# Block-recurrent attention with a gated MLP on one core: the next batch's M sets in pairs over four banks, the states' read next to the next scores

## The chip, the cores and the metric

The kernel runs on one core of a Trainium2 chip. The metric is the device time of one execution in microseconds; before the change it is 742.33 us (median of three runs, 742.26 to 742.41). The profiled execution has a span of 740.4 us, and the times inside it are counted from its start.

## The reference

Eight batches of eight heads; 512 tokens and 32 states of 64 numbers per head; everything in float32. Tokens read states, states read tokens, and both results go through an MLP whose activation is h * erf(softplus(h)):

```python
scores = scale * x @ state^T            # (512 x 32) per head
a      = softmax(scores)                # over the 32 states
xread  = a @ state                      # 512 rows of the batch
a2     = softmax(scale * state @ x^T)   # over the 512 tokens
sread  = a2 @ x                         # 32 more rows of the batch
h      = concat(xread, sread) @ w_in    # 512 -> 2048 (rows: heads side by side)
out    = (h * erf(softplus(h))) @ w_out # 2048 -> 512
```

## The kernel before

**M sets.** For the token rows xread is never formed. Since h = a (state w_in), the kernel forms the small matrices M = state w_in, once per batch, and then h = M^T a^T. One *M set* (`mixed`, L372, by way of `mixed_part`, L377) covers 512 columns of one batch's M: eight small matmuls (L385), each with 64 rows of a head pair's half (e = 0, 1) and 32 columns for one head pair i, so that eight of them fill the 128x128 array as tiles of 64x32. The results of e = 0 and e = 1 lie in two banks of the pool `ps_at`, and are copied out by ScalarE (L387) and VectorE (L388). A batch has four sets.

**Scores and read.** The scores of a batch (`scored`, L190, matmuls at L197) use the same 64x32 tiles; they need the transposed x, made by VectorE in `turn_x` (L330), and two `ps_at` banks, which ScalarE empties (L207). The states' read (`read_tokens`, L264) multiplies the turned token weights by x: 32 groups of matmuls 128 rows deep and 32 columns wide (L273) into one `ps_at` bank, which VectorE empties (L279). The weights for it come from an exponential on ScalarE (L246), and from VectorE's L248, L249 and L356, after which DMAs turn blocks.

**Hidden and output products.** The MLP runs in fast (seven-product) block schemes. `hidden7` (L437) forms a group of h from seven block products (L457, each four matmuls of 128 columns) in two banks p, q of the pool `ps_h`, then again in two more; ScalarE copies (L468, L473) and VectorE's additions (L465) empty them. Then come softplus (L464) and Erf (L507) on ScalarE and the multiplication by h on VectorE (L508). `project7` (L544) needs sums of these (S1 to S4, L559 to L562, VectorE) and adds up output blocks with matmuls of 256 columns (L563) in the four banks of `ps_o`; `store7` (L567) empties them with a copy on ScalarE (L574) and additions on VectorE (L573), and stores. `combine_m` (L397 to L400) and `combine_a` (L428 to L431) prepare sums of M and of the weights on VectorE; in batch 1 `combine_w` (L539) does so for w_out.

Accumulators: `ps_at` has two banks, `ps_h` two, `ps_o` four[...].

**The order.** From batch 1 on, each batch has four groups g. The matmuls of group g's `hidden7` and those of the previous group's `project7` are interleaved; `project7` is a generator that yields every second product of 256 columns, and `side` is a table from the number of such a step to small work put in at that point. With this table the next batch's attention is threaded in: `turn` is a generator over the stages of `attention` (scores; states' weights; token weights; normalisation and turning; read, with the load of the next x). Within this the tile scheduler may shift instructions a little; every engine then runs its own list in order. `behind` says that instructions are to be issued after the marked ones.

In the kernel before, group 0 of a batch has the batch's own read at step 2 and the next batch's scores at step 6, and groups 2 and 3 have one M set each at step 4 and at step 8.

Of the kernel before, what the change touches and what calls it, by code (L numbers as in the profile page):

```python
# [8 lines left out]
F32 = mybir.dt.float32  # L9
# [7 lines left out]
def kernel(  # L17
# [17 lines left out]
    nc = tc.nc  # L35
    B, H, S, D = x.shape
    Ns = state.shape[2]
    d_model, d_ff = moe_w_in.shape
    P = 128
    NI = H // 2  # L40
# [15 lines left out]
    mix = ctx.enter_context(tc.tile_pool(name="mix", bufs=4))  # L56
    act = ctx.enter_context(tc.tile_pool(name="act", bufs=2))
    outs = ctx.enter_context(tc.tile_pool(name="outs", bufs=2))
    ps_at = ctx.enter_context(tc.tile_pool(name="ps_at", bufs=2, space=PSUM))
    ps_h = ctx.enter_context(tc.tile_pool(name="ps_h", bufs=2, space=PSUM))  # L60
# [45 lines left out]
    st = const.tile([P, B, P], F32, name="st")  # L106
    x_t[0] = xin.tile([P, NC, H, D], F32, name="x")
    for c in range(NC):
        (nc.scalar, nc.sync)[c % 2].dma_start(
            out=x_t[0][:, c], in_=x[0, :, P * c:P * c + P].rearrange("h p d -> p h d"))  # L110
# [11 lines left out]
    w_in = const.tile([P, NF // 2, NK, 2 * P], F32, name="w_in")  # L122
# [29 lines left out]
    gw = GF * P  # L152
# [35 lines left out]
    marks = []  # L188
# [13 lines left out]
    def scores(b, xT):  # L202
        s2 = scored(b, xT)
        on_pe = marks.pop()
        sc = att.tile([P, 2, S], F32, name="sc")
        for e in range(2):
            last = nc.scalar.copy(sc[:, e], s2[e])  # L207
        marks[:] = last, on_pe
        return sc, last

    def states_weights(b, sc, both):

        aT[b] = keep.tile([P, 2, S], F32, name="aT")
        a = both[:, 0:2].rearrange("p e (k n) -> p e k n", n=Ns)
        m1 = small.tile([P, 2, NC * NI], F32, name="m1")
        for e in range(2):
            nc.vector.transpose(out=both[:, e], in_=sc[e])
        for e in range(2):
            nc.vector.reduce_max(out=m1[:, e], in_=a[:, e], axis=AX.X)
        for e in range(2):  # L220
            nc.vector.tensor_tensor(a[:, e], a[:, e], over(m1[:, e]), op=ALU.subtract)
            nc.scalar.activation(out=a[:, e], in_=a[:, e], func=ACTF.Exp, scale=scale)
        return a
# [11 lines left out]
    def largest(sc):  # L235
        m2 = small.tile([P, 2], F32, name="m2")
        for e in range(2):
            nc.vector.reduce_max(out=m2[:, e:e + 1], in_=sc[:, e], axis=AX.X)
        nc.vector.tensor_scalar(m2, m2, -scale, None, op0=ALU.mult)
        return m2  # L240
# [20 lines left out]

    sn_t = {}

    def read_tokens(b, a2T, z2):  # L264


        xt = x_t.pop(b)
        sr = ps_at.tile([P, 2, D], F32, name="at")
        for e in range(2):
            for c in range(NC):  # L270
                for i in reversed(range(NI)):
                    q = slice(Ns * i, Ns * i + Ns)
                    nc.tensor.matmul(out=sr[q, e, :], lhsT=a2T[:, e, c, q],  # L273
                                     rhs=xt[:, c, 2 * i + e, :],
                                     start=(c == 0), stop=(c == NC - 1))
        sn = sn_t[b] = const.tile([P, 2, D], F32, name="sn0") if b == 0 else \
            st[:, b - 1, :].rearrange("p (e d) -> p e d", e=2)
        for e in range(2):
            nc.vector.tensor_scalar(sn[:, e], sr[:, e], z2[:, e:e + 1], None, op0=ALU.mult)  # L279
# [48 lines left out]
    def turn_x(b):  # L328
        xT = att.tile([P, NI, S], F32, name="xT")
        last = nc.vector.transpose(out=xT.rearrange("p i t -> p (i t)"),  # L330
                                   in_=xq_t.pop(b).rearrange("p i m d -> p (i m d)"))
        if b + 1 < B:
            load_xq(b + 1)
        return xT, last

    def attention(b, xT=None):

        turned = []  # L340
        if xT is None:
            xT, *turned = turn_x(b)
        sc, _ = scores(b, xT)
        marks.extend(turned)
        yield
        both = att.tile([P, NI, S], F32, name="xT")
        a = states_weights(b, [sc[:, e] for e in range(2)], both)
        yield
        z2 = weigh_tokens(sc, largest(sc), both[:, 2:4])
        yield  # L350
        normalise(a)
        for e in range(2):
            nc.vector.transpose(out=aT[b][:, e], in_=both[:, e])
        yield

        nc.vector.transpose(out=both[:, 0:2], in_=both[:, 2:4])  # L356
        a2T = att.tile([P, 2, NC, P], F32, name="sc")
        blocks = both[:, 0:2].rearrange("p e (c m n) -> p m (e c) n", m=NI, n=Ns)
        rows = a2T.rearrange("p e c (i n) -> p i (e c) n", n=Ns)
        for m in range(NI):  # L360
            for i in range(NI):
                nc.sync.dma_start(out=rows[Ns * m:Ns * m + Ns, i],
                                  in_=blocks[Ns * i:Ns * i + Ns, m])
        yield
        read_tokens(b, a2T, z2)
        if b + 1 < B:
            load_x(b + 1)
        yield

    m_t = {}  # L370

    def mixed(b, g, *copies):  # L372

        m_t[b, g] = mix.tile([P, 2, gw], F32, name="m")
        mixed_part(b, g, 0, 1, *copies)

    def mixed_part(b, g, j, parts, copy0=nc.scalar.copy, copy1=nc.vector.tensor_copy):  # L377
        n = gw // parts
        mg = m_t[b, g][:, :, n * j:n * j + n]
        fs = slice(2 * g + j, 2 * g + j + 2 // parts)  # L380
        ps = [ps_at.tile([P, gw], F32, name="at")[:, 0:n] for _ in range(2)]
        for i in range(NI):
            for e in range(2):
                r, q = slice(D * e, D * e + D), slice(Ns * i, Ns * i + Ns)
                nc.tensor.matmul(out=ps[e][q, :], lhsT=st[r, b, q],  # L385
                                 rhs=w_in[r, fs, i, :], start=True, stop=True)
        copy0(mg[:, 0], ps[0])  # L387
        copy1(mg[:, 1], ps[1])  # L388
# [248 lines left out]
    def behind(marks, f, *args):  # L637
        with ExitStack() as order:
            for m in marks:
                order.enter_context(tc.issue_after(m.ins))  # L640
            return f(*args)
# [183 lines left out]
    xT, _ = turn_x(1)  # L825
# [6 lines left out]
    turn = attention(1, xT)  # L832
# [38 lines left out]
    at = [combine_a(1)]  # L871
# [12 lines left out]
    for b in range(1, B + 1):  # L884
        if b < B:
            groups = fast(b, 2, lambda h, b=b: put_x(b, h))
        else:
            groups = fast(b, 1, lambda h: put_s)
        for g, (first, second) in enumerate(groups):
            side = {}  # L890
            if b < B and g == 0:
                side[2] = lambda turn=turn: next(turn)
            if 1 < b < B and g == 0:
                side[3] = lambda: behind(marks, combine_m, b, 1 - begins(b))
            if b + 1 < B:

                late = b == 1
                if g == late:
                    turn = attention(b + 1)
                    side[6] = lambda: behind(marks, next, turn)  # L900
                if g == 1 + late:
                    side[1] = lambda: next(turn)
                    side[7] = lambda: behind(marks, lambda: [next(turn) for _ in range(3)])
                if g > 1:
                    o = g - 2 ^ begins(b + 1)
                    side[4] = lambda: mixed(b + 1, 2 * o)
                    side[8] = lambda: mixed(b + 1, 2 * o + 1)
                    if g == 3:
                        side[6] = lambda: behind(marks, combine_a, b + 1)
                        side[3] = lambda: behind(marks, combine_m, b + 1, begins(b + 1))  # L910
            elif b + 1 == B and g == 1:
                side[4] = lambda: [turn_read(range(k, min(k + 4, B))) for k in range(0, B, 4)]
            elif b + 1 == B and g > 1:

                if g == 2:
                    side[6] = lambda: combine_a(B)
                side[8] = lambda: combine_s(g - 2 ^ begins(B))
            steps = accompanied(pending(), side)
            copy = [nc.vector.tensor_copy] if (b, g) == (1, 1) else []
            gT_ = first(lambda: next(steps), *copy)  # L920
            if b == 1 and g == 0:
                combine_m(1, 1 - begins(1))
                behind(marks, combine_w, begins(1), 1, 2)
            if b == 1 and g == 1:
                behind(marks, combine_w, begins(1), 4, 3)
            done(steps)
            if b == 1 and g == 1:
                behind(marks, combine_w, 1 - begins(1), 1, 2, 4, 3)

            def pending(gT=gT_, second=second):  # L930
                return second(gT)
# [31 lines left out]
```

## Time and profile before

| what | value |
|---|---|
| time, median of 3 | 742.33 us |
| span of the profiled execution | 740.4 us |
| DMA, mean over the span | 63 GB/s |
| granted TensorE clock | 1.0 throughout |
| L385, M sets with 512 columns | 448 matmuls, 601 ns each, 31.5 us of busy time |
| L273, reads | 512 matmuls, 220 ns each, 8.8 us |
| L197, scores | 128 matmuls, 658 ns each, 10.6 us |

The counts are of instructions: a float32 product is two of them, so an M set has 16. In the rows of the groups the mean of one is its length from start to end; small matmuls on different tiles run side by side, which is why 448 of 601 ns make only 31.5 us. "PE" is TensorE's matmuls and "PEld" its weight loads, "DVE" VectorE, "ACT" ScalarE. In the chain of waits a piece is a line's stretch of work with its count, without time in which it only waited for its engine; a number in brackets behind a row of a timeline is the idle time ahead of it and what ended it.

### The profile page before, as it was taken

The page shows a single profiled execution, that of the slowest core. Times are in us where ns is not written, and L with a number is a line of the kernel's source. Part 1 is how long each engine was busy: PE and PEld are TensorE (multiplying, and loading weights), DVE is VectorE, ACT ScalarE, POOL GpSimd, SP SyncE. Part 2 cuts the span into 40 slices and gives each one's busy share as a digit, 9 for nine tenths or more (in the row PEclk, how much of TensorE's full clock was granted, in tenths as well). Part 3 has the DMA queues.
Part 4 walks back from the last instruction along what each step waited for, and adds up shares of the span by engine and source line. Part 5 has one row for each costly group of instructions (what it writes and reads, how often), then busy time and mean ns, then how long its engine had stood idle before and what let it go on. Part 6 is the DMA issues. An engine that isn't in the chain of part 4 may idle for free.

```text
span 740.4 us, 12067 instructions
## 1 busy us (share of the span) xinstructions
PE 727.6 (98%) x4986; PEld 583.9 (79%) x4986; DVE 523.5 (71%) x765; ACT 396.9 (54%) x498; POOL 0.7 (0%) x6
## 2 busy tenths in 40 slices
PE   7899999999999999999999999999999999999997
PEld 6434435878889888988889888988898889999996
DVE  3987888898688666966598568966596656575423
ACT  3898884656456445654365445654565434443340
POOL 0000000000000000000000000000000000000000
PEclk9999999999999999999999999999999999999999
DMA  7468752331160203310061105110201000000001
GB/s 231 170 205 250 209 101 58 86 58 26 33 130 19 53 1 76 69 29 29 15 128 21 38 1 111 35 35 22 59 29 29 30 1 29 1 29 1 27 4 28
DMA packets 139166, 46.40 MB, mean 63 GB/s; under 512 B 126696, under 2 KB 130536, under 8 KB 139112
## 3 DMA queue, kind: packets, MB, share of 16 engines
q1 hardware_dynamic: 136744, 44.78, 24.1%
q10 hardware_dynamic: 2368, 0.85, 0.5%
q8 instruction: 39, 0.64, 0.4%
q14 instruction: 15, 0.12, 0.1%
HBM read 33.03 MB, written 8.91 MB: 57 GB/s over the span
## 4 chain that ended last, share of the span: by engine, by line
PE 85%; DVE 2%; ACT 1%; issue 0%
PE o L563 49%; PE h L457 26%; PE at L385 4%; PE o L513 3%; PE h L673 1%; PE at L197 1%; PE at L273 1%; DVE s L508 1%; ACT s L507 0%; DVE hs L465 0%; ACT L507 0%; DVE raw L539 0%; DVE xT L356 0%; DVE ot L573 0%; PE at L285 0%
## 5 line engine op out<-in xcount | busy, mean ns | idle before, releaser
L464 ACT ACTIVATE s<-hs 128x512 f32<-128x512 f32 x120 | 75.4, 630 | 81.5 <-DVE hs L465 81.1
L563 PE MATMUL o<-w_out,s 128*128 128x256 f32 x480 | 118.2, 380 | 0.6 <-DVE s L508 0.4
L563 PE MATMUL o<-raw,hs 128*128 128x256 f32 x480 | 116.2, 384 | 0.0
L563 PE MATMUL o<-w_out,hs 128*128 128x256 f32 x480 | 114.8, 380 | 0.0
L563 PEld LDWEIGHTS o<-raw,hs 128*128 128x128 f32 x480 | 89.1, 190 | 32.0 <-issue 21.0
L563 PEld LDWEIGHTS o<-w_out,hs 128*128 128x128 f32 x480 | 90.6, 190 | 17.1 <-issue 4.2
L465 DVE TENSOR_TENSOR hs<-hs,h 128x512 f32<-128x512 f32 x90 | 61.8, 687 | 59.3 <-PE h L457 59.0
L465 DVE TENSOR_TENSOR hs<-s,h 128x512 f32<-128x512 f32 x60 | 41.0, 684 | 73.3 <-PE h L457 73.3
L563 PEld LDWEIGHTS o<-w_out,s 128*128 128x128 f32 x480 | 84.6, 191 | 8.9 <-DVE s L508 0.5
L457 PEld LDWEIGHTS h<-aT,m 128*128 128x128 f32 x672 | 83.9, 192 | 4.3 <-issue 1.4
L508 DVE TENSOR_TENSOR s<-s,hs 128x2048 f32<-128x2048 f32 x30 | 68.6, 2286 | 23.5 <-ACT s L507 23.5
L457 PE MATMUL h<-aT,m 128*128 128x128 f32 x672 | 84.6, 275 | 0.0
L468 ACT COPY s<-h 128x512 f32<-128x512 f32 x29 | 17.0, 585 | 100.5 <-PE h L457 100.5
L513 PE MATMUL o<-w_out,s 128*128 128x512 f32 x128 | 58.9, 600 | 0.3 <-DVE s L686 0.2
L457 PE MATMUL h<-sy,sx 128*128 128x128 f32 x448 | 59.1, 275 | 0.0
L457 PEld LDWEIGHTS h<-sy,sx 128*128 128x128 f32 x448 | 56.6, 192 | 1.8 <-issue 0.5
L507 ACT ACTIVATE s<-s 128x2048 f32<-128x2048 f32 x30 | 57.4, 1912 | 0.3
L563 PE MATMUL o<-raw,s 128*128 128x256 f32 x240 | 56.8, 379 | 0.0
L473 ACT COPY hs<-h 128x512 f32<-128x512 f32 x29 | 16.9, 582 | 73.5 <-PE h L457 73.5
L563 PEld LDWEIGHTS o<-raw,s 128*128 128x128 f32 x240 | 43.5, 190 | 4.8
L513 PEld LDWEIGHTS o<-w_out,s 128*128 128x128 f32 x128 | 23.1, 190 | 30.7 <-issue 26.2
L464 ACT ACT_TABLE_LOAD x31 | 39.8, 1283 | 0.6
(120 smaller groups left out, 912.5 us busy)
## 6 DMA issues: line engine op xcount, KB each, us to landing
raw<-in_moe_w_in_dram SPq DMA_DIRECT2D x8, 1024.0 KB, 5.4
raw<-in_moe_w_out_dram SPq DMA_DIRECT2D x8, 1024.0 KB, 4.7
xq<-in_x_dram SPq DMA_DIRECT2D x112, 64.0 KB, 2.1
x<-in_x_dram SPq DMA_DIRECT2D x56, 128.0 KB, 2.7
out_dram<-ot SPq DMA_DIRECT2D x18, 256.0 KB, 2.1
sc<-xT SPq DMA_DIRECT2D x112, 32.0 KB, 1.9
out_dram<-ot SPq DMA_DIRECT2D x28, 128.0 KB, 1.7
x<-in_x_dram ACTq DMA_DIRECT2D x2, 256.0 KB, 5.4
```

The costliest lines, as they stand in the source:

```text
L197: on_pe = nc.tensor.matmul(out=s2[e][q, :], lhsT=st[r, b, q], rhs=xT[r, i, :], start=True, stop=True)
L273: nc.tensor.matmul(out=sr[q, e, :], lhsT=a2T[:, e, c, q], rhs=xt[:, c, 2 * i + e, :], start=(c == 0), stop=(c == NC - 1))
L385: nc.tensor.matmul(out=ps[e][q, :], lhsT=st[r, b, q], rhs=w_in[r, fs, i, :], start=True, stop=True)
L457: last = nc.tensor.matmul(out=bank[:, q], lhsT=lhsT, rhs=rhs, start=(first and i == 0 and k == 0), stop=(i == GF - 1 and k == len(ops) - 1 ...
L464: nc.scalar.activation(out=s[:, k], in_=hs[:, k], func=ACTF.Softplus)
L465: add = lambda o, x, y: nc.vector.tensor_tensor(o, x, y, op=ALU.add)
L468: copy(m1, p)
L473: copy(c11, p)
L507: return (nc.scalar.activation(out=s, in_=s, func=ACTF.Erf), nc.vector.tensor_tensor(s, s, hs, op=ALU.mult))
L508: nc.vector.tensor_tensor(s, s, hs, op=ALU.mult))
L513: nc.tensor.matmul(out=acc[r], lhsT=gT[:, i, P * r:P * r + P], rhs=w_out[:, GF * g + i, :], start=(g == 0 and i == 0), stop=(g == NG - 1 a ...
L563: nc.tensor.matmul(out=acc[bank][:, E2 * c:E2 * c + E2], lhsT=lhs[:, i, :], rhs=rhs[:, g, i, :], start=(first and i == 0 and c == 0), stop ...
```

## The change

Two things are moved. First, the M sets are formed in pairs: `mixed_pair` allocates two `ps_at` banks and two `ps_h` banks, issues the sixteen small matmuls of two sets in a row, and then empties the four banks, ScalarE taking the e = 0 halves and VectorE the e = 1 halves. It stands at step 5 of groups 2 and 3 of batches 1 to 6, in place of one set at step 4 and one at step 8. Second, the read of batches 2 to 6 leaves step 2 of group 0 and is put at step 6, right in front of the next batch's scores; it takes a bank of `ps_h`, so that both banks of `ps_at` are left to the scores. Both aim at fewer changes of TensorE between its full array and its small tiles. The number of matmuls, copies and transfers stays the same.

In the changed kernel the set's matmul is L387 and its copies are L390 (ScalarE) and L391 (VectorE); of the other lines, those after the inserted function are 16 higher than before (L457 is L473, L465 is L481, L508 is L524, L563 is L579, L573 is L589).

```diff
-    def read_tokens(b, a2T, z2):
+    def read_tokens(b, a2T, z2, pool=ps_at, name="at"):
         xt = x_t.pop(b)
-        sr = ps_at.tile([P, 2, D], F32, name="at")
+        sr = pool.tile([P, 2, D], F32, name=name)
...
-        read_tokens(b, a2T, z2)
+        read_tokens(b, a2T, z2, *((ps_h, "h") if 1 < b < B - 1 else ()))
...
+    def mixed_pair(b, gs):
+
+        for g in gs:
+            m_t[b, g] = mix.tile([P, 2, gw], F32, name="m")
+        ps = [[pool.tile([P, gw], F32, name=n) for _ in range(2)]
+              for pool, n in ((ps_at, "at"), (ps_h, "h"))]
+        for k, g in enumerate(gs):
+            for i in range(NI):
+                for e in range(2):
+                    r, q = slice(D * e, D * e + D), slice(Ns * i, Ns * i + Ns)
+                    nc.tensor.matmul(out=ps[k][e][q, :], lhsT=st[r, b, q],
+                                     rhs=w_in[r, 2 * g:2 * g + 2, i, :], start=True, stop=True)
+        for k in 0, 1:
+            nc.scalar.copy(m_t[b, gs[k]][:, 0], ps[k][0])
+            nc.vector.tensor_copy(m_t[b, gs[k]][:, 1], ps[k][1])
...
-            if b < B and g == 0:
+            if b in (1, B - 1) and g == 0:
                 side[2] = lambda turn=turn: next(turn)
...
                 if g == late:
+                    side[6 if late else 6] = (lambda: behind(marks, next, turn)) if late else \
+                        lambda old=turn: (next(old), behind(marks, next, turn))
                     turn = attention(b + 1)
-                    side[6] = lambda: behind(marks, next, turn)
...
                 if g > 1:
                     o = g - 2 ^ begins(b + 1)
-                    side[4] = lambda: mixed(b + 1, 2 * o)
-                    side[8] = lambda: mixed(b + 1, 2 * o + 1)
+                    side[5] = lambda: mixed_pair(b + 1, (2 * o, 2 * o + 1))
```

## The prediction

> **What bounds the kernel now.** I read the page's busy shares first, then the chain that ended last, then that chain in order of time in the middle of the run, then TensorE's waits.
>
> ```profile
> PE 727.6 (98%) x4986; PEld 583.9 (79%) x4986; DVE 523.5 (71%) x765; ACT 396.9 (54%) x498; POOL 0.7 (0%) x6
> PE 85%; DVE 2%; ACT 1%; issue 0%
> ```
>
> TensorE is busy nearly everywhere and owns the chain. After 100 us the view of its waits lists only two, 0.4 us (for L508) and 0.3 us (for L573). So what counts is how long TensorE's stream itself is, and where a new wait could enter it. One batch of the chain in order of time (start, length, what):
>
> ```profile
> 487.40 1.73 PE o L563 x8
> 489.12 1.02 PE at L385 x16
> 490.14 3.65 PE o L563 x16
> 493.80 1.02 PE at L385 x16
> 494.81 3.65 PE o L563 x16
> ...
> 527.19 0.87 PE o L563 x4
> 528.05 1.03 PE at L273 x64
> 529.08 1.09 PE h L457 x8
> 530.17 3.89 PE o L563 x18
> 534.06 1.02 PE at L197 x16
> 535.08 4.95 PE o L563 x22
> ...
> 548.84 0.89 PE h L457 x8
> 549.73 8.64 PE o L563 x40
> ```
>
> The last line is the undisturbed rate: 8.64/40 = 0.216 us per L563 instruction of 256 columns (a float32 product is two instructions, 0.432 us). Sixteen of them take 3.46 us, but after each M set (L385) they take 3.65: 0.19 more. The set itself is two rounds of eight small matmuls of 512 columns, at the same rate two times 0.43 = 0.86 us, and stands at 1.02: 0.16 more. So **one excursion from the full array to the 64x32 tiles and back costs 1.02 + 0.19 = 1.21 us, of which 0.35 us is entering and leaving.** The read (L273) gives 1.03 plus 1.09 - 0.89 = 0.20 behind it, 1.23 us; the scores (L197) 1.02 plus 4.95 - 22 x 0.216 = 0.20, 1.22 us.
>
> Batch 0 has the read directly in front of scores already (the timeline of TensorE):
>
> ```profile
> 89.49 1.10 PE L273 MATMUL at<-x,sc 128*32 128x64 f32 x64
> 90.52 1.04 PE L197 MATMUL at<-xT,st 64*32 64x512 f32 x2
> 92.53 1.09 PE L197 MATMUL at<-xT,st 64*32 64x512 f32 x14 [0.97 <-DVE sn L279]
> ```
>
> From the read's start to the scores' first matmul it is 1.03 us, as from a read to a full-array matmul (527.98 to 529.01 in the same view). But the rest of those scores waits a microsecond until L279 has emptied the "at" bank that the read had taken. That is the wait which the read's move to an "h" bank keeps away.
>
> **What the Trainium skill says.** "TensorEngine Tiling (Array Packing)", Key Properties: changing the tiling mode drains TensorE. The trace agrees: 0.35 us per round trip, whatever the tile shape. "TensorE: Matmul & The Clock Gate", Part 3: small tiles of one mode run at once, their starts some 4 ns apart; here eight of them take 0.5 us like one. "Perfetto Trace Analysis", Identifying the Most-Contended Engine: busy matmul time is no measure of distance from the best; indeed the 98% contains every drain.
>
> **The change part by part.**
>
> *Pairs.* Batches 1 to 6 form four sets each for the next batch, 24 L385 excursions in the stages that are touched; now 12 pairs. A pair has one entry and exit and four rounds. Its third and fourth round aren't in the trace before; lower end 0.43 us each (a round at the stream's rate: a pair is 1.21 + 0.86 = 2.07 us, saving 2.42 - 2.07 = 0.35), upper end, if the change of banks between the two sets drained the array once more, half a round trip on top, saving only about 0.17. The read's rounds, 64 matmuls in 16 rounds in 0.88 us, keep a steady 0.056 us, so I take 0.43.
>
> *The pair's waits.* The second set needs both "h" banks. In the stage at 487 us the last addition out of them (DVE L465) runs 487.43 to 488.12; the second set would start at 487.3 + 6 x 0.216 x 2 + 0.1 + 0.88 = 490.9. No wait. (These times, and those below, are from the timelines of VectorE and ScalarE; the orders are those of the changed program's instruction lists.) Emptying them: in the changed order ScalarE does both its copies behind Erf (ends 492.0), so by 493.2; VectorE does one copy ahead of L508 and one behind it (L508 ends 494.3), so by 495.0. The next group's products 1 and 6, queued for these banks, come 20 x 0.432 + 2.07 = 10.7 us after 487.3, at 498.0 and 498.9. Slack 3.0 us at least. VectorE and ScalarE have the same copies as before, two and two per pair.
>
> *The read before the scores.* For b = 2 to 6, five times, the read leaves its place amid the hidden products and joins the scores: apart 1.23 + 1.22 = 2.45, together 1.03 + 1.02 + 0.20 = 2.25, saving 0.20. Could the scores wait? They need xT from L330. Product 3 ends at 530.0, L330 at 533.72; scores come at 530.0 + 8 x 0.432 + 0.1 + 1.03 = 534.6: 0.9 us of slack, since the order keeps L330 ahead of L279 on VectorE. L279 now stands behind L508: L330 533.7, L398 to L400 535.4, L508 537.7, L279 538.2. The next group needs that bank at 530.0 + 8.64 + 2.25 = 540.9 at the earliest: 2.7 us of slack. Behind L279 are L217 and the L573 additions that free output banks; the first would end near 540.3 and is needed at 540.9 + 1.8 = 542.7. The load of the next x, now behind the read, is due 80 us later. All hidden.
>
> *The one tight stage*, batch 1, group 2, where VectorE still carries work of the weight sums:
>
> ```profile
> 162.99 0.97 PE at L385 x2
> 163.96 1.93 PE o L563 x8
> 165.89 1.11 PE at L385 x14
> ...
> 170.82 2.29 DVE s L508
> 173.11 0.60 DVE m L388
> 173.71 0.11 DVE z L248
> 173.82 1.15 DVE xT L356
> ```
>
> Here a set was torn in two, so two sets cost three excursions, about 3.6 us, and the pair takes 2.07: 1.5 us less. But the new order lets L563's S4 product follow product 3 at once, and L562 delivers S4 only at 163.58: about 0.4 us lost. And on ScalarE it puts one token exponential with its table ahead of Erf and the other behind both copies. From the last softplus (166.96): table 1.28, exponential 0.91, table 1.28, Erf 1.91, two copies 1.15, table 1.28, exponential 0.91, that is 175.7. L248 on VectorE waits for that (before: 173.66), and behind it stand L356 (1.24) and L573 (0.6), which frees the output bank that L563 waited for already: free at 177.9 instead of 177.4. TensorE, first 1.1 us ahead, gives all of it back: its first L563 of that group comes at 178.1 instead of 177.55 with 0.2 us more done ahead of it. **I put this pair at -0.3 us**; bounds +1.5 (nothing lost) and -1.5 (further copies held up).
>
> **Sum.** 11 x 0.35 + 5 x 0.20 - 0.3 = 3.85 + 1.0 - 0.3 = 4.6 us less: 742.3 - 4.6 = 737.7 us.
>
> **The rivals.** (a) The forecast, 737.7 us, 0.74. (b) The tight stage costs nothing: 742.3 - 3.85 - 1.0 - 1.5 = 736.0 us, 0.10; for it: the estimate hangs on a chain of eight rows, each of which can slip; against it: the chain is made of in-order engines. (c) Half is lost: a bank change drains (0.17 instead of 0.35, 1.9 us less gain), or the tight stage costs 1.5 us more: about 739.5 us, 0.11. Against it speaks the read's even rounds. (d) The "h" banks become the bound: copies queue behind Erf and L508, products 1 and 6 wait in each of 12 groups. At 0.8 us each this is 9.6 us against 4.9 saved: 747 us, slower; 0.05, since it must first eat 3 us of slack each time. A smaller form of it ends near no change.
>
> **Numbers.** (a), (b), (c) are faster, as none is within 1.5 us of 742.3: 0.95. Of (d) 0.02 fall near no change and 0.03 slower. The range takes (a) and (c) with their spread: 736.4 to 739.7; it leaves out (d) and most of (b).
>
> **What would show it.** Right: in the chain L387 stands x32 at about 1.9 us with one slow stretch of L563 behind it; L273 and L197 are adjacent without a wait between; TensorE's waits after 100 us stay under 2 us, the largest near 178 us for L589 (the old L573). Wrong: waits of products (L473) for L390, L391 or L279, or of L197 for L330; or a gap between a pair's two sets of over 0.1 us.

## The result and the profile after

The changed kernel takes 737.0 us, the median of four runs (736.88 to 738.79), against 742.33 us (742.26 to 742.41) for the kernel before on the same chip: a ratio of 0.9934, 95% interval 0.9917 to 0.9951. That is 5.3 us less; the prediction was 4.6 us less. The interval is wide because some runs of either kernel are about 1.5 us longer (7 of 41 of the kernel before in the series beside experiments 1 to 4, and one of the four here); the medians hardly move by it. The spans of the profiled executions are 740.4 and 735.1 us, the clock 1.0 in both.

The page after, first its busy times, then the head of the chain that ended last:

```profile
PE 720.8 (98%) x4986; PEld 586.1 (80%) x4986; DVE 524.3 (71%) x765; ACT 396.8 (54%) x499; POOL 0.7 (0%) x6
PE 83%; DVE 2%; SPq 1%; issue 1%; DMA 0%; DVEq 0%
```

The same 4986 matmuls, and 6.8 us less of PE's busy time. VectorE and ScalarE are within 1 us of before (ScalarE has one table load more, 499 instructions for 498); the weight loads, which run beside the matmuls, show 2.2 us more. The work on TensorE did not get less. What got less is the time in which TensorE counts as busy and only changes its mode. The chain in order of time shows where (start, length, what), in the stages that answer to those of the prediction:

```profile
486.25 1.02 PE at L387 x16
487.27 0.86 PE h L387 x16
488.12 6.24 PE o L579 x28
...
524.92 3.02 PE o L579 x14
527.94 1.03 PE h L273 x64
528.97 1.02 PE at L197 x16
529.99 5.38 PE o L579 x24
```

A pair stands as two sets in a row. The first costs 1.02 us, as a single set did; the second costs 0.86, twice a bare round of 0.43, with nothing for the change of banks. Behind them 28 L579 take 6.24 us, of which 28 x 0.216 = 6.05 is the undisturbed rate, so 0.19 is the way back. The pair costs 1.02 + 0.86 + 0.19 = 2.07 us; two sets apart cost 2 x 1.21. The read and the scores touch now, and one slow stretch follows (24 x 0.216 = 5.18, so 0.20): 1.03 + 1.02 + 0.20 = 2.25 us where they took 2.45 apart.

TensorE's waits from 100 us to 740 us (for whom: us, times, longest) are these:

```profile
PE o L579 <- DVE ot L589: 0.5, 1, 0.5
PE o L579 <- DVE s L524: 0.4, 1, 0.4
PE h L473 <- ACT s L484: 0.2, 1, 0.2
PE o L579 <- DVE hs L578: 0.2, 1, 0.2
```

The one for L524 (137 us) is the old one for L508. The other three are in batch 1's group 2; the kernel before had only 0.3 us there. The view lists a wait without the slower starts around it, so the sums were also made from each matmul's start to the next one's, less the usual distance of undisturbed ones. By this count the cost of all excursions after 100 us (42 before, 24 after) fell from 51.1 to 44.7 us, 6.4 us less. The waits rose from 1.6 to 2.8 us, 1.2 more, all of it in that group. The difference, 5.2 us, is the result but for 0.1.

### The profile page after: what moved, and what is told of

Same layout as the page of the kernel before. It is cut to its first block, busy times and chain, and to the rows that moved or that the text cites. A ratio compares the mean times of both kernels' runs of the same rounds, so it can differ in the third digit from the quotient of the medians.

```text
span 735.1 us, 12066 instructions
## 1 busy us (share of the span) xinstructions
PE 720.8 (98%) x4986; PEld 586.1 (80%) x4986; DVE 524.3 (71%) x765; ACT 396.8 (54%) x499; POOL 0.7 (0%) x6
## 4 chain that ended last, share of the span: by engine, by line
PE 83%; DVE 2%; SPq 1%; issue 1%; DMA 0%; DVEq 0%
PE o L579 48%; PE h L473 26%; PE o L529 3%; PE at L387 2%; PE h L387 1%; PE h L689 1%; PE at L197 1%; PE h L273 1%; SPq L72 1%; PE at L401 1%; DVE raw L555 0%; DMA out_dram<-ot 0%; DVE hs L481 0%; DVE w_out L555 0%; DVE xT L330 0%
## 5 line engine op out<-in xcount | busy, mean ns | idle before, releaser
L579 PE MATMUL o<-w_out,s 128*128 128x256 f32 x480 | 118.2, 380 | 0.9 <-DVE ot L589 0.5
L579 PE MATMUL o<-raw,hs 128*128 128x256 f32 x480 | 117.1, 382 | 0.0
L579 PE MATMUL o<-w_out,hs 128*128 128x256 f32 x480 | 114.0, 381 | 0.2 <-DVE hs L578 0.2
L579 PEld LDWEIGHTS o<-raw,hs 128*128 128x128 f32 x480 | 90.1, 190 | 22.4 <-issue 10.9
L481 DVE TENSOR_TENSOR hs<-hs,h 128x512 f32<-128x512 f32 x90 | 61.8, 688 | 63.6 <-PE h L473 63.6
L579 PEld LDWEIGHTS o<-w_out,hs 128*128 128x128 f32 x480 | 90.8, 190 | 16.7 <-issue 4.2
L579 PEld LDWEIGHTS o<-w_out,s 128*128 128x128 f32 x480 | 84.7, 191 | 9.1 <-DVE ot L589 0.7
L481 DVE TENSOR_TENSOR hs<-s,h 128x512 f32<-128x512 f32 x60 | 41.1, 685 | 67.5 <-PE h L473 67.1
L473 PEld LDWEIGHTS h<-aT,m 128*128 128x128 f32 x672 | 83.9, 192 | 4.6 <-issue 1.4
L473 PE MATMUL h<-aT,m 128*128 128x128 f32 x672 | 84.7, 276 | 0.2 <-ACT s L484 0.2
L524 DVE TENSOR_TENSOR s<-s,hs 128x2048 f32<-128x2048 f32 x30 | 68.6, 2287 | 19.9 <-ACT s L523 19.9
L484 ACT COPY s<-h 128x512 f32<-128x512 f32 x29 | 17.0, 585 | 113.3 <-PE h L473 113.3
L473 PE MATMUL h<-sy,sx 128*128 128x128 f32 x448 | 59.1, 275 | 0.0
L473 PEld LDWEIGHTS h<-sy,sx 128*128 128x128 f32 x448 | 56.6, 192 | 1.8 <-issue 0.5
L579 PE MATMUL o<-raw,s 128*128 128x256 f32 x240 | 56.8, 380 | 0.0
L579 PEld LDWEIGHTS o<-raw,s 128*128 128x128 f32 x240 | 43.6, 191 | 4.8
```

The costliest lines, as they stand in the source:

```text
L473: last = nc.tensor.matmul(out=bank[:, q], lhsT=lhsT, rhs=rhs, start=(first and i == 0 and k == 0), stop=(i == GF - 1 and k == len(ops) - 1 ...
L481: add = lambda o, x, y: nc.vector.tensor_tensor(o, x, y, op=ALU.add)
L484: copy(m1, p)
L524: nc.vector.tensor_tensor(s, s, hs, op=ALU.mult))
L579: nc.tensor.matmul(out=acc[bank][:, E2 * c:E2 * c + E2], lhsT=lhs[:, i, :], rhs=rhs[:, g, i, :], start=(first and i == 0 and c == 0), stop ...
```

## The experiments

Ten kernels were run, each beside the kernel before on the same chip, which had medians of 742.41 to 742.45 us there. All diffs are against the changed kernel.

**1. Pairs alone.** Read and scores are where they were before.

```diff
-        read_tokens(b, a2T, z2, *((ps_h, "h") if 1 < b < B - 1 else ()))
+        read_tokens(b, a2T, z2)
-            if b in (1, B - 1) and g == 0:
+            if b < B and g == 0:
...
-                    side[6 if late else 6] = (lambda: behind(marks, next, turn)) if late else \
-                        lambda old=turn: (next(old), behind(marks, next, turn))
                     turn = attention(b + 1)
+                    side[6] = lambda: behind(marks, next, turn)
```

> The pairs alone; the read of batches 2 to 6 is back amid the hidden products with an "at" bank. Drain theory (each trip of TensorE from the full array to the small tiles and back costs 0.35 us, and the order of the other engines hides everything but the stage in batch 1): five reads are excursions of their own again, 5 x 0.20 = 1.0 us more than with both, 738.0 us. Rival (the read's move carries the gain, for instance by giving VectorE time before the scores): 741 us or more.

Measured: 738.16 us (738.08 to 738.49), ratio 0.9937, 0.9922 to 0.9952. So the pairs, with what they gain and lose in the tight stage, bring 742.4 - 738.2 = 4.2 us.

**2. The moved read alone.** The sets are formed singly again.

```diff
-                    side[5] = lambda: mixed_pair(b + 1, (2 * o, 2 * o + 1))
+                    side[4] = lambda: mixed(b + 1, 2 * o)
+                    side[8] = lambda: mixed(b + 1, 2 * o + 1)
```

> The read's move alone; the M sets stand singly at steps 4 and 8 as before the change. Drain theory: 742.3 - 5 x 0.20 = 741.3 us. Rival (the read's move carries the gain): 738.5 us or less.

Measured: 741.41 us, ratio 0.9986, 0.9978 to 0.9994. That is 1.0 us, five times 0.20. The two parts add up: 4.2 + 1.0 = 5.2.

**3. Four banks, but not in a row.** Both sets of a pair keep their banks, and one step of L579 comes between them. This parts the change of mode from the other things that a pair brings: its place (but for that one step), its banks, and the place of its copies behind Erf.

```diff
+    def mixed_in(b, g, pool, name):
+        m_t[b, g] = mix.tile([P, 2, gw], F32, name="m")
+        ps = [pool.tile([P, gw], F32, name=name) for _ in range(2)]
...
-                    side[5] = lambda: mixed_pair(b + 1, (2 * o, 2 * o + 1))
+                    side[5] = lambda: mixed_in(b + 1, 2 * o, ps_at, "at")
...
+                side[6] = lambda then=then, o=o: (mixed_in(b + 1, 2 * o + 1, ps_h, "h"), then())
```

> As the changed kernel, with the same four banks for two M sets, but the second set one step later, so that two instructions pairs of L579 stand between the sets. Drain theory: 12 more round trips at 0.35 us, 737.0 + 4.2 = 741.2 us, with L387 rows x16 in the chain and slow stretches behind each. Rival (the gain is from the four banks, or from the copies' later place, not from the joined sets): 737.0 us.

Measured: 741.15 us, ratio 0.9983, 0.9977 to 0.999: 4.1 us slower than the changed kernel, and level with experiment 2. The chain in order of time (in this kernel the set is L399 and the output product L590):

```profile
488.96 1.02 PE at L399 x16
489.98 1.06 PE o L590 x4
491.04 1.02 PE h L399 x16
492.06 5.38 PE o L590 x24
```

Four L590 cost 1.06 us instead of 4 x 0.216 = 0.86, and the second set 1.02 instead of 0.86. These are 0.20 for leaving and 0.16 for entering, 0.35 us for a visit of four instructions to the full array. It is what "TensorEngine Tiling (Array Packing)", Key Properties, calls a drain on a change of tiling mode. The page gives no figure; here it is 0.35 us a round trip. As in the changed kernel, the view lists no wait of TensorE from 180 us on. So neither the four banks nor the later copies bring the gain, but the missing round trip.

**4. The read in an "at" bank again**, in its new place in front of the scores.

```diff
-        read_tokens(b, a2T, z2, *((ps_h, "h") if 1 < b < B - 1 else ()))
+        read_tokens(b, a2T, z2)
```

> As the changed kernel, but the read in front of the scores takes an "at" bank instead of an "h" bank. The scheduler then has half of the scores directly behind the read and the other half two products later, waiting for L279, which stands behind L524 on VectorE. Bank theory (the "h" bank is needed): the second half adds an excursion of 1.2 us (half a set takes as long as a whole one) and waits some 1.6 us for L279, so 2.9 us in each of five batches, 737.0 + 14 = 751 us. Rival (the wait is short or hidden, since the scores needn't be complete at once): 737 to 738 us, or 743 us with the excursions alone.

Measured: 743.05 us (742.88 to 744.28), ratio 1.0006, 0.9997 to 1.0014. The rival was right, and the theory of a long wait wrong. The "h" bank does decide the matter: without it the move is worse than not moving. But TensorE does not stand and wait. The timelines of TensorE and then of VectorE:

```profile
532.75 1.10 PE L273 MATMUL at<-x,sc 128*32 128x64 f32 x64
533.78 1.06 PE L197 MATMUL at<-xT,st 64*32 64x512 f32 x8
534.77 1.13 PE L579 MATMUL o<-w_out,hs 128*128 128x256 f32 x4
535.83 1.06 PE L197 MATMUL at<-xT,st 64*32 64x512 f32 x8
```

```profile
536.81 0.47 DVE L279 TENSOR_SCALAR st<-at,z 128x64 f32<-128x64 f32 x2
```

With one bank taken by the read, the scores' two halves must share the other. The scheduler puts L579 between them, and the second half, at 535.83, runs a microsecond before L279 begins to empty the read's bank (536.81). So it doesn't need VectorE; it follows ScalarE's copy of the first half (L207, 534.91 to 535.49), and the view of TensorE's waits from 180 us on lists none. The price is one more excursion. The read with the first half costs 2.22 us, the second half alone 1.19, together 1.16 more than 2.25, and five times that is 5.8 (measured 743.05 - 737.0 = 6.05).

**5. Batch 1's group 2 back to single sets**, which prices the tight stage by itself.

```diff
+                    if late and g == 2:
+                        side[4] = lambda: mixed(b + 1, 2 * o)
+                        side[8] = lambda: mixed(b + 1, 2 * o + 1)
+                    else:
-                    side[5] = lambda: mixed_pair(b + 1, (2 * o, 2 * o + 1))
+                        side[5] = lambda: mixed_pair(b + 1, (2 * o, 2 * o + 1))
```

> As the changed kernel, but batch 1, group 2 has its two M sets singly at steps 4 and 8 again. The recorded prediction put the pair in that stage at a loss of 0.3 us; if so this kernel is faster, 736.7 us. By the trace of the changed kernel its three drains and the second set's torn rounds cost 1.5 us more and the new waits for L578, L484 and L589 1.2 us less, so this kernel is slower: 737.3 us. A rival on which the stage would be free (the waits come from elsewhere): 738.5 us.

Measured: 737.42 us (737.31 to 737.51), ratio 0.9933, 0.9919 to 0.9946; span 735.5. TensorE's wait there is 0.3 us for L589 as before. So the pair in this stage is a small gain, and not the loss that was predicted. Its worth is 0.4 us by medians and by spans, but both ratios' intervals are wider than that, and 0.1 us of the difference of the spans is there before 108 us already. The size therefore rests on the sums from start to start: excursions 46.2 and waits 1.6 us here, 44.7 and 2.8 in the changed kernel, which is 0.3 us.

**6. A pair in two banks.** Both sets use "at" banks, so the second has to wait until the first is copied out.

```diff
-              for pool, n in ((ps_at, "at"), (ps_h, "h"))]
+              for pool, n in ((ps_at, "at"), (ps_at, "at"))]
```

> As the changed kernel, but both sets of a pair take the two "at" banks, so that the second set must wait for the first one's copies, and the "h" banks stay with the hidden products. Copy theory: ScalarE does those copies behind Erf only, 0.8 us after TensorE would come to the second set, and the pair's one round trip becomes two (0.35): 12 x 1.15 = 14 us more, 751 us. Rival (copies keep up, so two banks lose only the second round trip): 741 us.

Measured: 748.12 us (747.92 to 748.17), ratio 1.0076, 1.0063 to 1.009. TensorE's waits from 180 us on, and ScalarE's timeline with TensorE's in one such stage:

```profile
PE at L387 <- ACT m L390: 5.1, 11, 0.5
```

```profile
494.03 1.91 ACT L523 ACTIVATE s<-s 128x2048 f32<-128x2048 f32 x1
495.84 0.57 ACT L390 COPY m<-at 128x512 f32<-128x512 f32 x1
```

```profile
493.85 1.09 PE L387 MATMUL at<-w_in,st 64*32 64x512 f32 x16
494.87 1.13 PE L579 MATMUL o<-raw,hs 128*128 128x256 f32 x4
496.46 1.09 PE L387 MATMUL at<-w_in,st 64*32 64x512 f32 x16 [0.47 <-ACT m L390]
```

The cause was the expected one: the copy L390 stands behind Erf, and the second set behind the copy. So the four banks are needed, as a condition and not as the gain. As in experiment 4 the expected size was too high (14 us, 11.1 measured): with four L579 between the two sets a wait of 0.47 us is left of the expected 0.8. The sets cost 2.97 us with the wait instead of 2.07: 0.9 each and 9.8 for the eleven pairs outside the tight stage. Most of the rest lies in that one, where the second set is torn in two.

**7. Erf first in the tight stage.** The token exponentials of batch 1's group 2 are ordered behind Erf, to save the detour over another table.

```diff
+    erf_of = []
...
-                finish(*gT)
+                erf_of[:] = finish(*gT)[:1]
...
-                    side[7] = lambda: behind(marks, lambda: [next(turn) for _ in range(3)])
+                    side[7] = lambda late=late: behind(marks + (erf_of if late else []),
+                                                       lambda: [next(turn) for _ in range(3)])
```

> As the changed kernel, but in batch 1, group 2 the token exponentials (L246) are ordered behind Erf on ScalarE, so that Erf and L524 come 2.2 us earlier, and one table load less is done. Order theory (the new table load ahead of Erf makes the waits near 176 us): 736.3 us or less. Rival (VectorE's amount of work in the stage sets the output bank's release, L589, whatever the order): 737.0 us, with the wait for L589 still there and longer, since less is queued ahead of it.

Measured: 737.07 us, ratio 0.9933, 0.992 to 0.9945, no gain. The two waits for L484 and L589 turned into one, at 177.15 instead of 177.30; from start to start they cost 1.3 us in both kernels:

```profile
177.15 1.99 PE L579 MATMUL o<-w_out,s 128*128 128x256 f32 x8 [1.01 <-DVE ot L589]
```

VectorE's timeline shows why. With Erf earlier, L524 begins at 171.04 instead of 172.21, and L248 no longer waits for ScalarE. But two sums (L577, L576) now stand ahead of L589 on VectorE, 0.6 us each:

```profile
173.96 0.68 DVE L577 TENSOR_TENSOR hs<-s 128x512 f32<-128x512 f32 x1
174.56 0.16 DVE L248 TENSOR_SCALAR z<-z 128x2 f32<-128x2 f32 x1
...
175.83 0.67 DVE L576 TENSOR_TENSOR hs<-hs,s 128x512 f32<-128x512 f32 x1
176.42 0.68 DVE L589 TENSOR_TENSOR ot<-m,o 128x512 f32<-128x512 f32 x1
```

ScalarE's order is thus not alone in holding the output bank: what ScalarE gave was taken by the order on VectorE. No run keeps L589 ahead of these sums, so the worth of that stays open.

**8. The same two moves in batch 0.** Its read goes to an "h" bank, and batch 1's four M sets, formed in batch 0, become two pairs.

```diff
-            read_tokens(0, a2T, z2)
+            read_tokens(0, a2T, z2, ps_h, "h")
...
-    def mixed_pair(b, gs):
+    def mixed_pair(b, gs, copy1=nc.vector.tensor_copy):
...
-    mixed(1, 2 * begins(1), nc.scalar.copy, nc.scalar.copy)
...
-    mixed(1, 2 * begins(1) + 1, nc.scalar.copy, nc.scalar.copy)
+    mixed_pair(1, (2 * begins(1), 2 * begins(1) + 1), nc.scalar.copy)
...
```

> The same two moves carried into batch 0: the read of batch 0 takes an "h" bank (in the changed kernel the scores behind it wait and are torn in two rounds of their own, 4.25 us in all against 2.25 for an undisturbed read and scores), and the four M sets of batch 1 are formed as two pairs (2 x 0.35 us). If all reaches the end: 737.0 - 2.0 - 0.7 = 734.3 us. Rival (VectorE, at 96% of busy time between 140 and 170 us, absorbs what TensorE gains ahead of that stage): 736.5 to 737.0 us, with longer waits at 137 and 177 us. In between, 735.5 us, if VectorE's own idle time before 131 us shrinks too.

Measured: 737.44 us, ratio 0.9939, 0.9926 to 0.9951; nothing gained. The excursions did shrink: read and scores from 4.25 us (with the microsecond of waiting) to 2.25, each pair to 2.07, together 2.7 us. TensorE's waits from 90 us on have two new rows:

```profile
PE o L529 <- DVE s L702: 1.5, 1, 1.5
PE h L689 <- ACT xT L222: 0.9, 1, 0.9
```

From start to start these cost 2.8 us. In the changed kernel the same stretch has no wait for either line and its chain stays on TensorE; here it runs over VectorE and ScalarE (from L217 at 94.33 to L702 at 106.56), so a TensorE that arrives earlier only waits. The rival's mechanism was right, its place was not: it happens at 97 to 107 us, not between 140 and 177.

**9. The last weight sums on GpSimd.** If VectorE is what the tight stage waits for, its four last `combine_w` differences could go to an idle engine.

```diff
-    def combine_w(g, *ns):
+    def combine_w(g, *ns, on=nc.vector):
...
-        sub = lambda o, x, y: nc.vector.tensor_tensor(o[:, g], x[:, g], y[:, g], op=ALU.subtract)
+        sub = lambda o, x, y: on.tensor_tensor(o[:, g], x[:, g], y[:, g], op=ALU.subtract)
...
-                behind(marks, combine_w, 1 - begins(1), 1, 2, 4, 3)
+                combine_w(1 - begins(1), 1, 2, 4, 3, on=nc.gpsimd)
```

> As the changed kernel, but the last four differences of combine_w in batch 1 (L555, four of 1.2 us on VectorE at 150 to 155 us) are done by GpSimd, which is idle. If VectorE's amount of work in batch 1, group 2 makes TensorE's waits there (0.5 us for L578, 0.5 for L484, 0.8 for L589 with their refills), they shrink or go: 737.0 - 1.8 = 735.2 us. Rival (GpSimd is too slow for it or holds VectorE up, so that the products that read the differences wait): 738 us or more.

Measured: 746.13 us (745.45 to 747.02), ratio 1.0049, 1.0036 to 1.0061: 9.1 us slower than the changed kernel. The edit also drops `behind`, so the differences do not only change their engine: GpSimd starts them much earlier, one at 92.5 us and three from 120 us on, where VectorE made them from 150.5 us on. Timelines of GpSimd and of VectorE where the three run:

```profile
119.95 2.64 POOL L555 TENSOR_TENSOR w_out<-w_out 128x1024 f32<-128x1024 f32 x1 [25.14 <-DVE w_out L149]
122.55 5.55 POOL L555 TENSOR_TENSOR raw<-w_out,raw 128x1024 f32<-128x1024 f32 x2
```

```profile
120.42 2.73 DVE L414 TENSOR_TENSOR sx<-sx,m 128x512 f32<-128x512 f32 x1
123.07 2.84 DVE L415 TENSOR_TENSOR m<-m 128x512 f32<-128x512 f32 x1
125.83 2.82 DVE L416 TENSOR_TENSOR sx<-m,sx 128x512 f32<-128x512 f32 x1
128.57 0.41 DVE L444 TENSOR_TENSOR sy<-aT 128x256 f32<-128x256 f32 x1
```

VectorE's additions of 0.69 us last 2.7 to 2.8 us each while GpSimd subtracts, one of them for one of GpSimd's, and are back at their length when it is done. "SBUF — State Buffer", Who interferes with whom, says this of a VectorE instruction with two SBUF inputs against a GpSimd one that reads SBUF: a lock, not a sharing. The trace agrees with it. Each difference thus holds VectorE up by 2.0 to 2.2 us, more than the 1.22 us that VectorE takes to make it. TensorE then waits 4.8 us for L445, in its second product of that group, and loses 1.7 us more at a clock of 0.57 for 4 us (4 x 0.43), as the table by stages shows (PE busy is the first engine column, PEclk the granted clock):

```profile
124.00:129.00 5.00, 0.71 (x7) 0.52 (x5) 4.98 (x3) 1.03 (x2) 4.02 (x2) 1.00 0.32 53
129.00:133.00 4.00, 3.50 (x11) 2.61 (x12) 3.95 (x8) 0.00 (x0) 0.00 (x0) 0.57 0.36 135
133.00:140.00 7.00, 7.00 (x48) 5.57 (x47) 2.99 (x6) 3.76 (x5) 0.00 (x0) 1.00 0.00 0
```

Before this TensorE was 2.1 us behind the changed kernel's trace: 0.45 before the first difference began, the rest after it (at 92.6 us VectorE's L147 takes 2.73 instead of 0.68, and TensorE waits 0.95 us for L222 and 0.25 for L702). That makes 2.1 + 4.8 + 1.7 = 8.6 of the 8.7 us between the spans.

The question was about the tight stage, and there nothing was gained. The waits for L578 and L484 are gone, but the one for L589 is 1.5 us instead of 0.5; from start to start the stage's waits cost 1.8 us in both kernels. As in experiment 7 the sums (L576 to L578) now stand ahead of L589 on VectorE. What the differences cost on GpSimd at their old, later place was not run.

**10. Experiment 9 with the read of batch 1 moved too**, as in the other batches. These lines come on top of those of experiment 9.

```diff
-        read_tokens(b, a2T, z2, *((ps_h, "h") if 1 < b < B - 1 else ()))
+        read_tokens(b, a2T, z2, *((ps_h, "h") if b < B - 1 else ()))
-            if b in (1, B - 1) and g == 0:
+            if b == B - 1 and g == 0:
...
-                    side[6 if late else 6] = (lambda: behind(marks, next, turn)) if late else \
-                        lambda old=turn: (next(old), behind(marks, next, turn))
+                    side[6] = lambda old=turn: (next(old), behind(marks, next, turn))
```

> As the one before, and the read of batch 1 also goes to the scores that follow it, with an "h" bank. The scheduler leaves one product of L579 between the two, so the number of round trips is the same and the drain theory gives no gain from it: as the one before, 735.2 us. Rival (the read's place alone counts): 0.2 us or more less.

Measured: 747.95 us (746.84 to 748.21), ratio 1.0067, 1.0054 to 1.0081. It has the same 4.8 us wait; the clock stays near half until 136 us instead of 133, and products wait 0.6 us for L481, L579 0.7 for L524. Because its base had lost so much ahead of this place, the run doesn't tell what moving batch 1's read would bring in the changed kernel; that stays open.

No version was faster than the changed kernel.

## Why the prediction was right, and where it was off

- **What bounds the kernel**: TensorE's own stream, right. From 180 us on the view of waits lists none on it in the changed kernel, and the gain is the sum of the excursions that went, less the waits in batch 1.
- **The excursion, 1.21 us with 0.35 for entering and leaving**: right, and now shown by itself in experiment 3 (0.20 + 0.16). One detail differs: the eight matmuls of a round start about 7 ns apart in the trace, not 4, the figure that the prediction cites. The sum doesn't use that figure.
- **The pair, 2.07 us, saving 0.35 rather than 0.17**: 2.07 in every pair; the second set's 0.86 us are two bare rounds, so the change of banks within the same tiles costs nothing here.
- **The pair's waits on "h" banks, hidden by 3 us of slack**: right. No product waits for L390 or L391 after the change; in the stage at 486 us the last copy out of an "h" bank ends at 491.19 and the next group's first product starts at 494.20. Rival (d), these banks as the bound, needed waits that no stage shows; experiment 6 shows how they look where the banks are too few.
- **The read next to the scores, 0.20 us each, the scores not held up by L330**: right, 2.25 us and no gap in five of five.
- **The tight stage, -0.3 us**: the step that failed, though it is small beside the rest. It gained 0.3. The working had the gain right (a torn set and a whole one, measured 3.59, against 2.07, so 1.5 us) and the places of two waits (S4, then the output bank behind L589), but the loss was 1.2 and not 1.8 us. The first wait is as said, 0.5 us from start to start. A third wait, 0.2 us for L484, the copy behind the second exponential on ScalarE, was not in the prediction. The wait for L589 was forecast too late. ScalarE's timeline, then VectorE's and TensorE's:

```profile
168.14 0.72 ACT L246 ACTIVATE xT<-sc,m 128x512 f32<-128x512 f32 x1
...
168.97 1.28 ACT L523 ACT_TABLE_LOAD   x1
170.27 1.91 ACT L523 ACTIVATE s<-s 128x2048 f32<-128x2048 f32 x1
172.09 0.57 ACT L390 COPY m<-at 128x512 f32<-128x512 f32 x1
172.55 0.59 ACT L390 COPY m<-h 128x512 f32<-128x512 f32 x1
173.16 1.28 ACT L246 ACT_TABLE_LOAD   x1
174.45 0.72 ACT L246 ACTIVATE xT<-sc,m 128x512 f32<-128x512 f32 x1
```

```profile
172.21 2.29 DVE L524 TENSOR_TENSOR s<-s,hs 128x2048 f32<-128x2048 f32 x1 [1.39 <-ACT s L523]
174.54 0.69 DVE L575 TENSOR_TENSOR hs<-s 128x512 f32<-128x512 f32 x1
175.30 0.17 DVE L248 TENSOR_SCALAR z<-z 128x2 f32<-128x2 f32 x1
175.38 1.24 DVE L356 STREAM_TRANSPOSE xT<-xT 128x1024 f32<-128x1024 f32 x1
...
176.58 0.67 DVE L589 TENSOR_TENSOR ot<-m,o 128x512 f32<-128x512 f32 x1
```

```profile
163.51 1.99 PE L579 MATMUL o<-w_out,hs 128*128 128x256 f32 x8 [0.21 <-DVE hs L578]
...
176.06 0.71 PE L473 MATMUL h<-aT,m 128*128 128x128 f32 x4 [0.23 <-ACT s L484]
177.30 2.00 PE L579 MATMUL o<-w_out,s 128*128 128x256 f32 x8 [0.53 <-DVE ot L589]
```

  ScalarE's order is just the predicted one. But a copy of 0.57 us is followed by the next one after 0.46, Erf's 1.91 by the first copy after 1.82, and the exponential with its read-out takes 0.83 to the next start, not 0.91. So in these rows the next instruction starts before the record of the last one ends, and a sum of lengths is too long: over the eight rows it is 8.7 us where the trace has 8.4. This and a start 0.1 us earlier bring L248 to 175.30 instead of 175.7. From L248 to the end of L589 the prediction put 2.2 us, more than the two rows that it names add up to (1.84); measured are 1.95 (177.25, not 177.9). TensorE's first L579 follows 0.05 us later, not 0.2: at 177.30, not 178.1. ScalarE's chain also binds only narrowly: on VectorE L575 stands right ahead of L248, and such an addition is followed after 0.6 us, so without any wait for ScalarE L248 could have begun at about 175.14. With +0.3 for this term the sum is 3.85 + 1.0 + 0.3 = 5.15 us, against 5.3 measured. Of the prediction's rivals, (b) had put this term at +1.5 and (c) further down; it lies between (a) and (b).
- **What would show it**: the pair of 1.9 us (as two rows of 16, 1.02 and 0.86, since the two sets lie in different pools), the two lines next to each other and TensorE's waits (1.3 us in the view, the largest at 177.3 for L589) are all there.

## What to carry to other kernels

Where TensorE is busy nearly all the time, count its changes between the full array and small tiles as well as its matmuls: joining two visits saves a fixed amount each time, and it is real only if there are banks enough that the second half needn't wait for the first to be emptied. Ask which engine empties them and what stands ahead of it there. A stage in which VectorE and ScalarE carry the chain can give such savings back, 1.2 of 1.5 us in batch 1's group 2 and all of 2.7 in batch 0. A chain of rows like those of ScalarE here is priced from start to start, not by adding their lengths; and when one engine is relieved, look again at what order the scheduler then gives to the other.

## What the runs showed of the hardware

- Half a set on small tiles costs as much as a whole one: in experiment 4 eight score instructions (one e, so 64 of the array's rows) with their entry and exit cost 1.19 us, sixteen on all rows 1.22. So a set torn into halves pays for two full visits.
- Going from 128x32 tiles straight to 64x32 tiles is 0.2 us cheaper than going through the full array (2.25 against 2.45 us), but not free: the first score set behind a read still takes 1.02 us and not 0.86.
- After five microseconds in which TensorE was busy for 0.71 us its clock fell to about 0.57 for some 4 us (experiment 9). "TensorE: Matmul & The Clock Gate", Part 1, describes such a halving after an idle window; here the wait of 4.8 us cost 1.7 us on top of itself.
- GpSimd's 128x1024 float32 subtraction lasts 2.4 to 2.7 us, and an addition with two SBUF inputs that VectorE starts beside it ends only some 0.6 us after it (123.15 after 122.59 us), about an addition's own length. VectorE's L147, which reads a single tile, is held up in the same way (2.73 us instead of 0.68).
